# Gated linear attention feeding a feed-forward block: outputs of two head pairs at a time, a quarter of the TensorE array per head for the carried states

## The chip, the cores and the metric

The kernel runs on one core of a Trainium2 chip. The metric is the device time of one launch in microseconds (us), as the median of several runs. TensorE is called PE, VectorE DVE, ScalarE ACT, GpSimd POOL, SyncE SP.

## The reference

```python
def _attn_ref(q, k, v, f_logit):                       # each (4, 8, 768, 48)
    f = 1.0 / (1.0 + np.exp(-f_logit))
    for t in range(S):
        state = f[:, :, t, :, None] * state + np.einsum('bhd,bhe->bhde', k[:, :, t], v[:, :, t])
        y[:, :, t] = np.einsum('bhd,bhde->bhe', q[:, :, t], state)

def _moe_ref(x, w_in, w_out):                          # (3072, 384), (384, 2048), (2048, 384)
    h = x @ w_in
    g = np.where(h >= 1, h, np.where(h <= -1, 0.0, (h + 1) ** 2 / 4.0))
    return g @ w_out
```

The first part is a recurrence over 768 positions with a 48 x 48 state for each of 4 batches and 8 heads; its outputs, all heads side by side, are the rows x of the second part.

## The kernel before

**Steps, pairs, units.** The 768 positions are cut into 6 *steps* (`NI`) of 128. In each step the 8 heads are 4 *pairs* (`NP`), the two heads of a pair on rows 0 to 47 and 64 to 111 of a tile. Batches (`B` = 4) lie side by side in the free dimension. The feed-forward block of a step is 16 *units* (`NJ`) of 128 hidden columns. Unit u of the whole kernel (0 to 95) is IN, nine matmuls of x with `w_in` (line 205, tile `ph`), then the activation on ACT and DVE, then OUT, nine matmuls with `w_out` (line 229, tile `po`). Weights and x are split into a rounded high part and a remainder (`w_hi`, `w_lo`), hence three products for each.

**The attention of a pair in one step.** `gate` scans the forget gates on DVE (lines 399, 406) and multiplies k and q by them (408, 410). `scores` makes k·q for each head and batch (line 456), each on half of the array's rows, and `masks` multiplies by a triangle on DVE (467, tile `am`). `outputs` makes, for each batch, values times masked scores (line 514, one matmul for each head, each on half of the array's columns) and, from step 1 on, the carried state times q (lines 517 and 518, over all 112 rows against a block-diagonal tile `dbd`, again one half of the columns each). `states` makes k·v for the next step (564) from the transposed keys `kn`, transposed on PE (480) in steps 0 and 1 and on DVE (494) later. The decayed states are written into `dbd` by two DVE operations for a pair (441), one for each head; the new state is the sum of it and of `states`' result, two DVE operations (571).

**From outputs to x.** An output is rounded by ACT (528, the high part) and the remainder is made by DVE (544). In step 0 it is done otherwise: the output is computed a second time (521), PE subtracts the high part (540, tile `minus`) and ACT writes the remainder (541). The fourth pair has no row block of its own in x: its outputs go to tile `y3`, and six DMAs (`move`, half of them issued by SP and half by ACT; `x<-y` in the profile) carry them to rows 48 to 63 and 112 to 127 of the three x tiles. The first unit of a step waits for these six DMAs (`need = moved[i]`).

**Weights.** The weights arrive as 24 pieces of 64-bit words (`raw<-in_w`). Each is put together on DVE (308, 311, 313) and split into the high part (ACT, 322 or 320) and the remainder: on DVE (323), or, for every second piece from the seventh on, by an accumulating DMA issued on POOL (319). Units 0 to 3 need the first three pieces for IN, the next three for OUT, and so on.

**What sets the order.** Every operation is put into a `Plan` with a cost in ns (`COST`); a list scheduler gives each a start and the instructions are emitted in order of start, a fixed queue for each engine. PE's own order is the order of the calls. Where the plan leaves PE without work for over 0.7 us, `warm` puts in matmuls of zeros (line 283) for 0.7 of it. The calls of `scores` and `outputs` are put between units by a table:

```python
        at = 16 * (i - 1) + ((5, 8, 11, 14) if i == 1 else (1, 5, 9, 13))[m]
        before = 16 * (i - 1) + ((2, 5, 8, 11) if i == 1 else (-2, 1, 5, 9))[m]
```

`before` is the unit after which the pair's scores stand, `at` that after which its outputs and states stand. In steps 2 to 5 three of the four outputs of a step thus follow another pair's scores directly.

## Time and profile before

| | us |
|---|---|
| median of 3 runs | 520.79 |
| lowest and highest run | 518.71, 520.99 |
| the profiled execution's own time | 519.36 |
| its span, first to last instruction | 517.3 |

The granted TensorE clock of the profiled execution is 0.994 of full speed. In a page's rows `L205` is line 205, `ph<-x,w_hi` says which tile is written from which, and `x576` is the number of records. A matmul of plain fp32 operands (lines 456 to 564) leaves two records, one for each of its two passes; one of rounded operands (205, 229) leaves one. PEld is the weight load that goes ahead of a matmul. Times within the execution are counted from its first instruction.

### The profile page before, as it was taken

To read this page: it belongs to the slowest core of one execution; us is meant where nothing else is said; L and a number is where in the kernel's file an instruction comes from. 1 tells how busy PE (TensorE), PEld (TensorE's weight loads), DVE (VectorE), ACT (ScalarE), POOL (GpSimd) and SP (SyncE) were. 2 spreads that over 40 slices of the span, in tenths; PEclk is the share of its full clock that TensorE was granted. 3 is DMA by queue.
4 is the path that set the end of the run, shared out by engine and by line. 5 is a ranking of instruction groups with operands and counts; after the bars stand their busy time and mean duration, and the time that the engine had idled before them with its cause. 6 is when DMAs were issued, how large, how long until landed. Compare 5 with 4: busy or idle time off the path is not lost.

```text
span 517.3 us, 8421 instructions
## 1 busy us (share of the span) xinstructions
PE 501.5 (97%) x3295; PEld 407.0 (79%) x3295; DVE 390.6 (76%) x768; ACT 238.8 (46%) x389; POOL 31.0 (6%) x57
## 2 busy tenths in 40 slices
PE   7979999999999999999999999999999999999995
PEld 3747878887887888888888888888888888888883
DVE  7999999999999999998898798865655443433332
ACT  2347665654343453454443543534434434544542
POOL 3111111021100100010100010100000000000000
PEclk9899999999999999999999999999999999999999
DMA  8689687825401204412304512145522311100001
GB/s 283 200 238 322 182 250 195 240 71 132 129 25 52 77 22 97 158 29 91 116 24 117 163 58 98 41 140 154 177 90 82 114 50 30 63 1 1 0 1 67
DMA packets 22367, 56.65 MB, mean 110 GB/s; under 512 B 3504, under 2 KB 7088, under 8 KB 22320
## 3 DMA queue, kind: packets, MB, share of 16 engines
q1 hardware_dynamic: 19872, 51.31, 31.0%
q0 software_dynamic: 1296, 2.36, 2.8%
q10 hardware_dynamic: 1152, 2.37, 2.0%
q8 instruction: 28, 0.46, 0.4%
q14 instruction: 19, 0.16, 0.1%
HBM read 44.22 MB, written 4.72 MB: 95 GB/s over the span
## 4 chain that ended last, share of the span: by engine, by line
PE 76%; DVE 17%; DMA 4%; issue 1%; ACT 0%; SPq 0%; ACTq 0%; DVEq 0%
PE po L229 33%; PE ph L205 31%; PE pa L456 4%; PE pa L514 3%; DVE kn L494 3%; PE pa L518 3%; DMA raw<-in_w 2%; DVE glo L223 2%; DVE bits L313 2%; DVE bits L311 2%; DVE act L217 1%; DMA v<-in_v 1%; DVE am L467 1%; DVE w L399 1%; DVE w_lo L323 1%
## 5 line engine op out<-in xcount | busy, mean ns | idle before, releaser
L205 PE MATMUL ph<-x,w_hi 128*128 128x512 f32 x576 | 177.4, 389 | 0.0
L209 ACT ACTIVATE act<-ph,half 128x512 f32<-128x512 f32 x96 | 66.2, 689 | 145.1 <-PE ph L205 138.4
L205 PEld LDWEIGHTS ph<-x,w_hi 128*128 128x128 f32 x576 | 108.1, 188 | 22.5
L229 PE MATMUL po<-ghi,w_lo 128*128 128x512 f32 x288 | 115.8, 402 | 1.1 <-DMA w_lo<-bits 0.8
L205 PE MATMUL ph<-x,w_lo 128*128 128x512 f32 x288 | 112.4, 390 | 2.4 <-DMA x<-y 2.4
L217 DVE SCALAR_TENSOR_TENSOR act<-ph,act 128x512 f32<-128x512 f32 x96 | 65.9, 686 | 63.3 <-ACT act L212 62.8
L229 PE MATMUL po<-ghi,w_hi 128*128 128x512 f32 x288 | 112.5, 390 | 0.0
L220 ACT CAST ghi<-act 128x512 fp32r<-128x512 f32 x96 | 59.6, 620 | 82.0 <-DVE act L217 80.0
L229 PE MATMUL po<-glo,w_hi 128*128 128x512 f32 x288 | 83.2, 390 | 0.3 <-DVE glo L223 0.3
L223 DVE TENSOR_TENSOR glo<-act,ghi 128x512 fp32r<-128x512 f32 x96 | 65.9, 687 | 20.5 <-ACT ghi L220 19.1
L229 PEld LDWEIGHTS po<-ghi,w_lo 128*128 128x128 f32 x288 | 54.0, 188 | 15.3 <-ACT ghi L220 1.6
L205 PEld LDWEIGHTS ph<-x,w_lo 128*128 128x128 f32 x288 | 54.1, 188 | 14.2 <-DMA x<-y 2.9
L229 PEld LDWEIGHTS po<-glo,w_hi 128*128 128x128 f32 x288 | 53.9, 188 | 12.5 <-DVE glo L223 1.0
L229 PEld LDWEIGHTS po<-ghi,w_hi 128*128 128x128 f32 x288 | 54.1, 188 | 10.3
L212 ACT ACTIVATE act<-act 128x512 f32<-128x512 f32 x96 | 60.7, 632 | 2.9
L494 DVE STREAM_TRANSPOSE kn<-kq 32x128 f32<-32x128 f32 x192 | 58.1, 303 | 2.9
L467 DVE TENSOR_TENSOR am<-pa,mask 128x512 f32<-128x512 f32 x45 | 30.7, 686 | 17.1 <-PE pa L456 13.8
L514 PE MATMUL pa<-am,v 128*48 128x128 f32 (+1 forms) x368 | 36.8, 277 | 0.1
L517 PE MATMUL pa<-kq,dbd 112*64 112x128 f32 x160 | 30.6, 272 | 0.0
L518 PE MATMUL pa<-kq,dbd 112*48 112x128 f32 x160 | 30.6, 272 | 0.0
L456 PEld LDWEIGHTS pa<-kq 48*128 48x128 f32 x360 | 22.4, 188 | 8.9 <-issue 5.3
L456 PE MATMUL pa<-kq 48*128 48x128 f32 x360 | 27.0, 285 | 1.6 <-DVE kq L410 1.6
(87 smaller groups left out, 418.6 us busy)
## 6 DMA issues: line engine op xcount, KB each, us to landing
raw<-in_w SPq DMA_DIRECT2D x48, 512.0 KB, 3.5
kq<-in_kq SPq DMA_DIRECT2D x18, 512.0 KB, 4.5
v<-in_v SPq DMA_DIRECT2D x24, 192.0 KB, 4.0
out_y<-raw SPq DMA_DIRECT2D x18, 256.0 KB, 2.7
f<-in_f SPq DMA_DIRECT2D x16, 256.5 KB, 3.0
w_lo<-bits POOLq DMA_DIRECT2D x9, 256.0 KB, 5.2
kq<-kq ACTq DMA_DIRECT2D x18, 64.2 KB, 2.9
kq<-kq SPq DMA_DIRECT2D x18, 64.2 KB, 2.5
```

What stands on the lines that cost most here:

```text
L205: nc.tensor.matmul(ps, w_in(part, j, kt), xt[:, kt, t], start=(n == 0), stop=(n == 8))
L209: nc.scalar.activation(a, ps, AF.Relu, bias=half, scale=0.5)
L212: nc.scalar.activation(a, a, AF.Square)
L217: nc.vector.scalar_tensor_tensor(out=a, in0=ps, scalar=1.0, in1=a, op0=ALU.max, op1=ALU.min)
L220: nc.scalar.copy(hi, a)
L223: nc.vector.tensor_tensor(out=lo, in0=a, in1=hi.bitcast(F32), op=ALU.subtract)
L229: nc.tensor.matmul(po[e], w_out(part, j, e), g, start=(j == 0 and n == 0), stop=(j == NJ - 1 and n == 2))
L456: nc.tensor.matmul(ps[:, b], kt[a:z, B - 1 - b], qt[a:z, b], start=True, stop=True)
L467: o = vec("dve", lambda t=t, ps=ps: nc.vector.tensor_tensor(out=t, in0=ps, in1=mask.rearrange("u (o t) -> u o t", o=1).broadcast_to([C, B, ...
L494: nc.vector.transpose(kn[n % 2][u:u + 32, :, r:r + 32], src[:, :, u:u + 32])
L514: nc.tensor.matmul(ps[r:z, m], vb[:, a:a + z - r], t[:, m], start=True, stop=first)
L518: nc.tensor.matmul(ps[64:R, m], dt[:, m, 64:R], qt[:, m], start=False, stop=True)
```

## The change

- The heads are paired anew (`PAIRS`), so that two pairs give two whole x tiles: the first heads of both pairs one, the second heads the other.
- `outputs` is called once for two pairs. For each batch, four matmuls take the carried states with q: each 48 rows by 64 (or 48) columns, one for each head of the two pairs, in a quarter of the array each. Then come the values with the masked scores of all four heads, two columns' halves at a time as before.
- `states` is called once for two pairs, with 64 columns for a pair's first head; the new states of both pairs are one sum on DVE instead of four.
- `dbd` goes; the decayed states stand compactly in `ds`, written by one operation for a pair instead of two.
- In step 0 the second computation of the outputs, `minus` and the gathering DMAs go. `heads` computes the outputs of heads 0 to 5 straight into the three x tiles' layout, `thirds` adds the 16-column thirds of heads 6 and 7 there by 32-column matmuls, with one tiny closing matmul of zeros for each tile. The remainder is made by DVE, as in later steps. Values of step 0 come in two layouts of their own (`va`, 512 KB; `vb`, 640 KB); later steps load the values of two pairs in one DMA of 384 KB.
- The first unit waits for the three x tiles one at a time instead of for the DMAs.
- The table moves: scores of step 1 stand after units 2, 4, 8, 10 and its outputs after 7 and 13; from step 2 on scores after -2, 0, 5, 7 and outputs after 3 and 11, counted from the step before's first unit. Plan costs change, and zeros are put in where the plan leaves PE without work for over 0.5 us, for 0.9 of it.

```diff
+
+PAIRS = ((0, 2), (1, 3), (4, 6), (5, 7))
+
-COST = dict(mm=227, scores=1100, y0=1850, y=1850, states=500, turn=500, rows=317, scan=1145, dve=605, small=200, state=365,
+COST = dict(mm=227, scores=1100, y=2600, states=900, turn=500, rows=317, scan=1145, dve=605, small=200, state=300, sums=480,
...
-    v = tiles(4, [C, B, 2, D], F32, "v")
+    v_all = const.tile([C, 2 * B * 4 * D], F32, name="v")
+    v = [v_all[:, k * B * 4 * D:(k + 1) * B * 4 * D].rearrange("u (b h e) -> u b h e", b=B, h=4) for k in range(2)]
-    am = tiles(3, [C, B, C], F32, "am")
+    am = tiles(4, [C, B, C], F32, "am")
     kn = tiles(2, [C, B, C], F32, "kn")
-    dbd = tiles(2, [R, B, R], F32, "dbd")
-    state = const.tile([R, NP * B, D], F32, name="state")
+
+    sd = const.tile([128, NP * B * D + 2 * B * D + 16], F32, name="sd")
+    state, ds = sd[:R, 0:NP * B * D].rearrange("r (g e) -> r g e", e=D), sd[:R, NP * B * D:]
     act_f = tiles(2, [128, N + 1], F32, "act")
...
-    minus = const.tile([R, R], F32R, name="minus")
...
-    set_dbd = [add("POOL", 700, lambda t=t: fresh(t)) for t in dbd]
+    set_ds = add("POOL", 200, lambda: fresh(ds[:, 2 * B * D:]))
...
-    def bank(first):
-
-        count = 6 if first else 3
-        k = turn["n"] % count
-        turn["n"] += 1
+    def bank(k=None):
+
+        if k is None:
+            k = turn["n"] % 3
+            turn["n"] += 1
...
+    va = sd[:, 0:4 * B * 64].rearrange("u (b h e) -> u b h e", b=B, h=4)
+    vb = v_all[:, 0:B * 320].rearrange("u (b e) -> u b e", b=B)
...
-        c["lv"] = dma(v[n % 4], vv[i, p], 192, old(n - 4, "y", "st"))
+        if n % 2:
+            c["lv"] = att[n - 1]["lv"]
+        elif i == 0:
+            c["lv"] = dma(va if p == 0 else vb, vad if p == 0 else vbd, 512 if p == 0 else 640)
+        else:
+            c["lv"] = dma(v[k], vv[i, p // 2], 384, old(n - 4, "y", "st"), att[2]["st"])
...
-            for a, z in HEADS:
-                c["db"].append(vec("state", lambda a=a, z=z: nc.vector.tensor_tensor(
-                    out=dbd[k][a:z, :, a:z], in0=state[a:z, p * B:(p + 1) * B],
-                    in1=whole(kq[p])[a:z].rearrange("r (b o) -> r b o", o=1).broadcast_to([z - a, B, D]), op=ALU.mult),
-                    pf, state_of[i - 1, p], old(n - 2, "y", "se"), set_dbd[k]))
-
-    def scores(n):
+            c["db"].append(vec("state", lambda: nc.vector.tensor_tensor(
+                out=ds[:, n % 2 * B * D:(n % 2 + 1) * B * D].rearrange("r (b e) -> r b e", b=B), in0=state[:, p * B:(p + 1) * B],
+                in1=whole(kq[p])[:R].rearrange("r (b o) -> r b o", o=1).broadcast_to([R, B, D]), op=ALU.mult),
+                pf, state_of[i - 1, p // 2], old(n - 2, "y", "se"), set_ds))
...
+    def scores(n, at=(None, None)):
-        held = [bank(i == 0) for _ in HEADS]
+        held = [bank(k) for k in at]
...
-            t = am[(2 * n + h) % 3]
+            t = am[n % 2 * 2 + h]
-                c["sc"], ready["mask"], old(n - 2 + h, "y"))
+                c["sc"], ready["mask"], old(n - 2, "y"))
...
+    def rounded(b, yf, hi, lo, y, past):
+        eh = sca("act", lambda: nc.scalar.copy(hi, yf), y, past)
+        el = vec("dve", lambda: nc.vector.tensor_tensor(out=lo, in0=yf, in1=hi.bitcast(F32), op=ALU.subtract), eh)
+        banks[b] = [eh, el]
+        return [eh, el]
+
+        held = [bank(), bank()]
...
+        def emit():
+
+            for m in range(B):
+                for e, h in ((0, 0), (1, 1), (1, 0), (0, 1)):
+                    (r, z), q = HEADS[h], part(kq[p + e], 1)
+                    a = (e * B + m) * D
+                    nc.tensor.matmul(held[h][1][64 * e:(64, R)[e], m], ds[r:z, a:a + (64, 48)[e]], q[r:z, m], start=m == 0, stop=False)
+
+            for h, (_, ps, _) in enumerate(held):
+                for m in range(B):
+                    vm = vt[:, m].rearrange("u h e -> u (h e)")
+                    nc.tensor.matmul(ps[0:64, m], vm[:, h * D:h * D + 64], am[h][:, m], start=False, stop=m == B - 1)
+                    nc.tensor.matmul(ps[64:R, m], vm[:, (2 + h) * D:(3 + h) * D], am[2 + h][:, m], start=False, stop=m == B - 1)
+
+        y = c["y"] = d["y"] = add("PE", "y", emit, c["am"], d["am"], c["lv"], c["db"], d["db"], [b[2] for b in held])
+        xt = x[i % 2]
+        for t, (b, ps, _) in zip((p, p + 1), held):
+            hi, lo = (y3[:, 0], y3[:, 1]) if t == NT else (xt[:, t, 0], xt[:, t, 1])
+            past = [moved.get(i - 1)] if t == NT else [unit_in.get((i - 2, NJ - 1))]
+            x_of[i, t] = rounded(b, wide(ps)[:R], hi[:R], lo[:R], y, past)
+        if p > 0:
+
+            moved[i] = [move(k, xt[r:r + 16, t].bitcast(F32), y3[z + 16 * t:z + 16 * t + 16].bitcast(F32), x_of[i, NT], x_of[i, t])
...
+        def emit():
+            for e in range(2):
+                for m in range(B):
+                    for h, (r, z) in enumerate(((0, 64), (64, R))):
+                        a = (e * B + m) * D
+                        nc.tensor.matmul(ps[r:z, a:a + D], kn[e][:, B - 1 - m, r:z], vs[e][h](m), start=True, stop=True)
...
+        s = state[:, p * B:(p + 2) * B].rearrange("r b e -> r (b e)")
+        if i == 0:
+            o = sca("copy", lambda: nc.scalar.copy(s, ps[:R, 0:2 * B * D]), c["st"])
+        else:
+            o = vec("sums", lambda: nc.vector.tensor_tensor(out=s, in0=ps[:R, 0:2 * B * D], in1=ds[:, 0:2 * B * D], op=ALU.add),
+                    c["st"], c["db"], d["db"])
+        c["se"] = d["se"] = banks[b] = state_of[i, p // 2] = [o]
...
+    def heads(t, vs, a, deps, held=None):
+
+        ps = firsts[t][1]
         def emit():
             for m in range(B):
+                for e in range(2):
+                    nc.tensor.matmul(ps[64 * e:64 * e + 64, m], vs(m, e), a[e][:, m], start=m == 0, stop=False)
+
+        return add("PE", 870, emit, deps, held)
+    def thirds(t, a, deps):
...
+                for e in range(2):
+                    w = vb[:, m, 128 + 96 * e + 32 * t:160 + 96 * e + 32 * t]
+                    nc.tensor.matmul(ps[64 * e + 32:64 * e + 64, m], w, a[e][:, m], start=False, stop=False)
+
+            nc.tensor.matmul(ps[:, B - 1, C - 1:], zeros, zeros[:, 0:1], start=False, stop=True)
...
-        need = moved[i] if j == 0 else []
+        need = moved[i] if j == 0 and i > 0 else []
...
+        if u == 0:
+
+            n = 0
+            for kt in range(3):
+                for k, terms in ((0, ((w_lo, 0), (w_hi, 0))), (1, ((w_hi, 1),))):
+                    def some(kt=kt, terms=terms, n=n):
+                        for k, (part, t) in enumerate(terms):
+                            nc.tensor.matmul(s, w_in(part, j, kt), x[0][:, kt, t], start=(n + k == 0), stop=(n + k == 8))
+                    o = add("PE", len(terms) * COST["mm"], some, x_of[0, kt][k], split[kt])
+                    n += len(terms)
+            unit_in[i, j] = o
...
-    ready["minus"] = sca(200, lambda: nc.scalar.mul(minus, ident[:R, :R], -1.0), ready["ident"])
         prepare(n)
-        scores(n)
-        if n > 0:
-            outputs(n - 1)
-        if n > 1:
-            remainder(n - 2)
-        masks(n)
-    outputs(NP - 1)
-    remainder(NP - 2)
+        scores(n, ((0, 1), (2, 3), (0, 1), (3, 0))[n])
+        if n == 1:
+            for t in range(2):
+                att[0]["y"] = att[1]["y"] = heads(t, lambda m, e, t=t: va[:, m, 2 * e + t], am[t::2], [att[e]["am"][t] for e in range(2)], att[0]["lv"])
+        transpose_tensor(n, (1, 3)[n])
+    two = [att[n]["am"] for n in (2, 3)]
+    heads(2, lambda m, e: vb[:, m, 64 * e:64 * e + 64], am[0::2], [a[0] for a in two], [att[2]["lv"], att[1]["am"]])
+    for t in range(NT):
+        y = att[2]["y"] = att[3]["y"] = thirds(t, am[1::2], [a[1] for a in two])
+        x_of[0, t] = rounded(firsts[t][0], wide(firsts[t][1]), x[0][:, t, 0], x[0][:, t, 1], y, None)
+        u = 16 * (i - 1)
+        groups.setdefault(u + ((2, 4, 8, 10) if i == 1 else (-2, 0, 5, 7))[m], []).append((0, n))
+        if m % 2 == 0:
+            groups.setdefault(u + ((7, 13) if i == 1 else (3, 11))[m // 2], []).append((1, n))
...
-        if u == 1:
+        if u == 0:
+            states(0)
+        elif u == 1:
             for n in (2, 3):
                 transpose_tensor(n)
-            for n in (2, 3):
-                states(n)
+        elif u == 2:
+            states(2)
...
-                if o is unit_in[0, 0]:
-
-                    warm(int((o.start - idle) / 230) + 4)
-                elif idle and o.start - idle > 700:
-                    warm(int((o.start - idle) * 0.7 / (330 if o.start < 50000 else 230)))
+                if idle and o.start - idle > 500:
+                    warm(int((o.start - idle) * 0.9 / (330 if o.start < 10000 else 230)))
...
```

The order of PE's instructions before, in step 2: the end of one pair's outputs and its states, between the IN of one unit and the OUT of another (`pa` is the output bank, `v` values, `am` masked scores).

```order
L514 MATMUL pa_115<-am_81,v_73 64x128
L514 MATMUL pa_115<-am_79,v_73 48x128
L517 MATMUL pa_115<-kq_69,dbd_85 64x128
L518 MATMUL pa_115<-kq_69,dbd_85 48x128
L564 MATMUL pa_113<-v_73,kn_83 48x48 x8
L229 MATMUL po_118<-ghi_92,w_lo 128x512
```

PE's instructions of the change at the outputs of two pairs: one batch of each kind, and the first two of the states (`sd` holds the decayed states).

```order
L537 MATMUL pa_110<-kq_68,sd 64x128
L537 MATMUL pa_108<-kq_69,sd 48x128
L537 MATMUL pa_110<-kq_69,sd 48x128
L537 MATMUL pa_108<-kq_68,sd 64x128
...
L542 MATMUL pa_110<-am_76,v 64x128
L543 MATMUL pa_110<-am_78,v 48x128
...
L570 MATMUL pa_109<-v,kn_80 64x48
L570 MATMUL pa_109<-v,kn_80 48x48
```

Before, the four rows of lines 514 to 518 stand four times for one pair, so 32 matmuls for two pairs, and 16 for their states. In the change there are 16 of line 537, then 16 of lines 542 and 543, then 16 of line 570, in one block.

PE's instructions before, from the end of step 0's outputs to the first unit (`minus` is the negated identity, `ident,kq` the transposes).

```order
L540 MATMUL pa_114<-x_89,minus 112x512
L283 MATMUL ph_117<-zeros 128x512
L540 MATMUL po_118<-y_91,minus 112x512
L480 MATMUL po_119<-ident,kq_68 128x112 x4
L480 MATMUL po_120<-ident,kq_69 128x112 x4
...
L564 MATMUL pa_113<-v_72,kn_82 64x48
...
L205 MATMUL ph_116<-x_89,w_lo 128x512
```

The same place in the change.

```order
L500 MATMUL pa_109<-ident,kq_68 128x112 x4
...
L592 MATMUL pa_110<-am_76,v 64x128
...
L603 MATMUL po_114<-am_77,v 32x128
...
L605 MATMUL po_114<-zeros 128x1
L603 MATMUL po_115<-am_77,v 32x128
...
L605 MATMUL pa_110<-zeros 128x1
L629 MATMUL ph_111<-x_85,w_lo 128x512
L629 MATMUL ph_111<-x_85,w_hi 128x512 x2
```

The transposes now stand ahead of the last outputs, the first states behind the first unit, and the first unit follows the last of the `thirds` directly.

PE's instructions of the change in step 1's first scores and the OUT of unit 1 behind them; before, the transpose, the scores and the OUT stood there with no row of line 283 among them.

```order
L500 MATMUL pa_109<-ident,kq_68 128x112 x4
L287 MATMUL po_115<-zeros 128x512
...
L480 MATMUL pa_110<-kq_68 128x128
...
L233 MATMUL po_115<-ghi_89,w_hi 128x512
L287 MATMUL po_115<-zeros 128x512
...
L233 MATMUL po_113<-glo_91,w_hi 128x512
```

From the first unit to the OUT of unit 13 the change has 36 matmuls of zeros (two of them inside the first unit); before had none. From there to the end it has 4, and before had 6.

More of the change, by code (lines that the diff above doesn't have):

```diff
@@ L137, in gla_moe @@
 @with_exitstack
-def gla_moe(ctx: ExitStack, tc: tile.TileContext, ff, kqd, f0, vv, wd, maskd, identd, gates, values, headsd, out):
+def gla_moe(ctx: ExitStack, tc: tile.TileContext, ff, kqd, f0, vv, vad, vbd, wd, maskd, identd, gates, values, headsd, out):
     nc = tc.nc
@@ L496, in transpose_rows @@
         c["tr"] = c["kn"][-1]
+    def rounded(b, yf, hi, lo, y, past):
[3 more added lines that the diff above has]
+        return [eh, el]
     def outputs(n):
         i, p = pairs[n]
-        c = att[n]
-        b, ps, held = bank(i == 0)
-        first = i == 0
-        ms = [am[(2 * n + h) % 3] for h in range(2)]
-        qt, dt = part(kq[p], 1)[:R], dbd[n % 2]
@@ L523, in outputs @@
-        c["y"] = add("PE", "y0" if first else "y", emit, c["am"], c["lv"], c["db"], held, again and again[2])
-        xt = x[i % 2]
-        hi, lo = (y3[:, 0], y3[:, 1]) if p == NP - 1 else (xt[:, p, 0], xt[:, p, 1])
-        yf = wide(ps)
-        past = [moved.get(i - 1)] if p == NP - 1 else [unit_in.get((i - 2, NJ - 1))]
-        eh = sca("act", lambda: nc.scalar.copy(hi[:R], yf[:R]), c["y"], *past)
-        c["rest"] = b, again, yf[:R], hi[:R], lo[:R], eh
-        if not first:
-            remainder(n)
@@ L533, in remainder @@
-    def remainder(n):
-        i, p = pairs[n]
-        b, again, yf, hi, lo, eh = att[n]["rest"]
-        xt = x[i % 2]
-        if again:
-            y = wide(again[1])[:R]
-            o = add("PE", 300, lambda: nc.tensor.matmul(y, minus, hi, start=False, stop=True), eh, ready["minus"])
-            el = sca("act", lambda: nc.scalar.copy(lo, y), o)
-            banks[b], banks[again[0]] = [eh], [el]
-        else:
-            el = vec("dve", lambda: nc.vector.tensor_tensor(out=lo, in0=yf, in1=hi.bitcast(F32), op=ALU.subtract), eh)
-            banks[b] = [eh, el]
-        x_of[i, p] = [eh, el]
-        if p == NP - 1:
-            moved[i] = [move(k, xt[r:r + 16, t].bitcast(F32), y3[z + 16 * t:z + 16 * t + 16].bitcast(F32), eh, el, x_of[i, t])
-                        for t in range(NT) for k, (r, z) in enumerate(((48, 0), (112, 64)))]
@@ L561, in emit @@
+    firsts = [bank(k) for k in (4, 5, 2)]
+    def heads(t, vs, a, deps, held=None):
+        ps = firsts[t][1]
         def emit():
             for m in range(B):
-                for h, (r, z) in enumerate(rows):
-                    nc.tensor.matmul(ps[r:z, m, :D], kn[n % 2][:, B - 1 - m, r:z], v[n % 4][:, m, h], start=True, stop=True)
-        c["st"] = add("PE", "states", emit, c["kn"], c["lv"], held)
-        s = state[:, p * B:(p + 1) * B]
-        if i == 0:
-            c["se"] = [sca("copy", lambda: nc.scalar.copy(s, ps[:R, :, :D]), c["st"])]
-        else:
-            c["se"] = [vec("state", lambda r=r, z=z: nc.vector.tensor_tensor(
-                out=s[r:z], in0=ps[r:z, :, :D], in1=dbd[n % 2][r:z, :, r:z], op=ALU.add), c["st"], c["db"]) for r, z in HEADS]
```

85 lines of the change are left out of this document (43 added, 42 removed).

## The prediction, made before the change was run

> **What bounds the kernel now.** First the top of the page and its two rows of tenths, then two stretches (busy time of PE, PEld, DVE, ACT and POOL, granted clock, DMA share, GB/s), then PE's waits.
>
> ```profile
> span 517.3 us, 8421 instructions
> ...
> PE 501.5 (97%) x3295; PEld 407.0 (79%) x3295; DVE 390.6 (76%) x768; ACT 238.8 (46%) x389; POOL 31.0 (6%) x57
> ...
> PE   7979999999999999999999999999999999999995
> ...
> DVE  7999999999999999998898798865655443433332
> ```
>
> ```profile
> 100.00:120.00 20.00, 20.00 (x158) 16.61 (x154) 19.79 (x36) 10.69 (x18) 3.51 (x4) 1.00 0.49 136
> ...
> 320.00:360.00 40.00, 40.00 (x274) 33.16 (x273) 27.40 (x54) 17.92 (x28) 1.31 (x2) 1.00 0.33 98
> ```
>
> ```profile
> PE ph L205 <- DMA x<-y: 2.4, 1, 2.4
> ...
> PE po L229 <- DMA w_lo<-bits: 0.8, 1, 0.8
> ```
>
> There are three stages. Until the first unit PE waits and is filled with zeros; the longest wait is for the gathered outputs. From there to about 120 us PE and DVE are both full (20.00 and 19.79 of 20). After that PE alone is full and DVE has room (27.4 of 40). So a PE microsecond saved late is a microsecond of the total; one saved at the start is worth it only as far as DVE follows.
>
> **The late stage, steps 2 to 5.** PE's rows at a pair's outputs and states alone, at scores alone, and in the last step at the last pair's outputs:
>
> ```profile
> 191.12 0.61 PE L205 MATMUL ph<-x,w_hi 128*128 128x512 f32 x2
> 191.66 0.43 PE L514 MATMUL pa<-am,v 128*64 128x128 f32 x4
> ...
> 193.25 0.27 PE L518 MATMUL pa<-kq,dbd 112*48 112x128 f32 x1
> 193.25 0.27 PE L517 MATMUL pa<-kq,dbd 112*64 112x128 f32 x1
> 193.36 0.27 PE L518 MATMUL pa<-kq,dbd 112*48 112x128 f32 x1
> 193.37 0.27 PE L517 MATMUL pa<-kq,dbd 112*64 112x128 f32 x1
> 193.47 0.53 PE L564 MATMUL pa<-v,kn 128*48 128x48 f32 x16
> 193.93 0.50 PE L229 MATMUL po<-ghi,w_lo 128*128 128x512 f32 x1
> 194.26 0.40 PE L229 MATMUL po<-ghi,w_hi 128*128 128x512 f32 x1
> ```
>
> ```profile
> 198.23 1.16 PE L456 MATMUL pa<-kq 48*128 48x128 f32 x16
> 199.32 0.50 PE L229 MATMUL po<-ghi,w_lo 128*128 128x512 f32 x1
> ```
>
> ```profile
> 430.84 0.43 PE L514 MATMUL pa<-am,v 128*64 128x128 f32 x4
> ...
> 432.75 0.50 PE L229 MATMUL po<-ghi,w_lo 128*128 128x512 f32 x1
> ```
>
> The chain of waits gives the blocks in which scores and outputs stand together, with states and, in the last step, without:
>
> ```profile
> 212.63 1.09 PE pa L456 x16
> 215.98 2.27 PE po L229 x9
> 218.25 2.04 PE ph L205 x9
> ...
> 411.37 1.09 PE pa L456 x16
> 414.37 2.26 PE po L229 x9
> ```
>
> Scores alone take 1.09 (198.23 to 199.32), outputs and states alone 2.27, of which the outputs 1.81 and the states 0.46; all three 3.35 (212.63 to 215.98); without states 3.00, and the last pair's outputs 1.91. Each interruption also costs about 0.2 at its edges: 0.31 from the start of the last IN matmul (191.35, the second of the two) to 191.66, and 0.33 from 193.93 to 194.26, where nine undisturbed matmuls take 2.04, 0.23 each. Steps 2 to 4 each have five interruptions: 1.09 + 3 x 3.35 + 2.27 + 5 x 0.2 = 14.4. The last has 1.09 + 3 x 3.00 + 1.91 + 1.0 = 13.0.
>
> The change has six interruptions, four of scores and two of outputs. In the rows of lines 517 and 518 both column halves start a pass together, 0.11 apart from pass to pass: a slot. Two pairs now need 16 slots for values (1.81, as for one pair before) and, for the carried states, 16 matmuls of two passes in four quarters: 8 slots, 0.88, if the quarters run side by side; before, the two pairs had 16. A change of array form adds some 0.2: the scores' 8 slots are 0.88 but take 1.09. The states of two pairs have the form of step 0's, first head 64 wide:
>
> ```profile
> 32.65 1.13 PE L564 MATMUL pa<-v,kn 128*64 128x48 f32 x32 [1.23 <-ACT kn L483]
> 33.71 2.55 PE L283 MATMUL ph<-zeros 128*128 128x512 bf16 x11
> ```
>
> These 32 passes take about 1.0 (32.65 to 33.71 with the edge), where twice 0.46 stood before: the wider weights give nothing back. The block's two output banks are held until ACT and DVE have rounded both tiles; `states` takes the third bank, and the next scores stand two or more units later, so nobody waits for that. A block is 0.88 + 0.2 + 1.81 + 0.95 = 3.85, a step 4 x 1.09 + 2 x 3.85 + 6 x 0.2 = 13.3, so three steps save 1.1 each; the last step has 4.36 + 2 x 2.9 + 1.2 = 11.4 and saves 1.6. Zeros: 6 before, 4 now, at 0.23 each (11 in 2.55): 0.5. Together 3.3 + 1.6 + 0.5 = 5.4. The gather in these steps now starts after unit 11 instead of 13 and stays hidden. The unknown is the quarters: no row has them. At no gain at all (16 slots) the late stage loses 8 blocks x 0.88 of it, 7.0, and ends 1.6 worse than now; nothing below 8 slots is possible, since each quarter has 8 passes.
>
> The Trainium skill, "TensorE: Matmul & The Clock Gate", Part 3 on packing small matmuls, says that matmuls start and end strictly in program order. By that rule a matmul's second pass would hold up the next quarter's first, two quarters would work at a time, and these 16 matmuls would take 16 slots, 1.76. The trace speaks against it as far as two halves show it: the order has line 517 first, yet at 193.25 a pass of 518 starts, ahead of the second pass of 517 at 193.37. No run here shows quarters in any order, so the rule stays as a rival.
>
> **The start.** Before, in step 0:
>
> ```profile
> 22.73 1.16 PE L456 MATMUL po<-kq 48*128 48x128 f32 x14 [0.34 <-ACT x L541]
> ...
> 29.09 0.48 PE L540 MATMUL po<-y,minus 112*112 112x512 f32 x1
> ...
> 38.65 0.50 PE L205 MATMUL ph<-x,w_lo 128*128 128x512 f32 x1 [2.39 <-DMA x<-y]
> ```
>
> From the last remainder's matmul to the first unit lie 9.6 us: a copy, six DMAs and their landing. They go. The last scores end at 23.9 in both (the gather of k and q ahead of them stays). What then follows, with these durations:
>
> ```profile
> L467 DVE TENSOR_TENSOR am<-pa,mask 128x512 f32<-128x512 f32 x45 | 30.7, 686 | 17.1 <-PE pa L456 13.8 <-PE pa L514 3.2
> L528 ACT CAST x<-pa 112x512 fp32r<-112x512 f32 x17 | 9.9, 585 | 4.1 <-PE pa L518 4.1
> L544 DVE TENSOR_TENSOR x<-pa,x 112x512 fp32r<-112x512 f32 x15 | 10.2, 678 | 0.0
> ```
>
> Two masks (0.69 each) end at 25.4. The third of the `heads` and the three `thirds` are 8 slots each and a change of form, 1.1: with two transposes in front they start near 25.5 and end at 30.0. Rounding the last tile takes 0.59 + 0.68 and two hand-overs, so the first unit, which waits for the tiles one by one, ends near 32.0. Before it ended at 38.65 + 2.04 = 40.7. Gain 8.7; earliest 31 (no change of form), latest 35, if the masks stand behind pieces on DVE, or the third piece's high part behind the two key copies that now stand ahead of it on ACT.
>
> **Step 1 gives most of that back.** OUT of unit 13 waits for one of the last pieces:
>
> ```profile
> 115.84 0.68 DVE L323 TENSOR_TENSOR w_lo<-bits,w_hi 128x512 fp32r<-128x512 f32 x1
> ...
> 116.63 0.50 PE L229 MATMUL po<-ghi,w_lo 128*128 128x512 f32 x1
> ```
>
> The piece is ready at 116.52, PE starts 0.11 later, at the end of its own queue. Both are full. From unit 0's end PE has 27 more INs and OUTs (nine at 2.04, 55.1) and 75.9 in all (40.7 to 116.63), so 20.8 of attention. The change has there five scores (6.5), two double blocks (8.1), 24 transposes (2.4, a slot each), step 0's states in two pieces (2.3) and 34 zeros at 0.23 (7.8): 27.1, 6.3 more. OUT of unit 13 comes at 32.0 + 55.1 + 27.1 = 114.2. The zeros stand for waits on DVE that the plan foresees, and cover 0.9 of them; the tenth that is left, 0.8, I add: 115.0, 1.6 earlier than before.
>
> DVE could follow that far. Its rows:
>
> ```profile
> L441 DVE TENSOR_TENSOR dbd<-state,kq 48x192 f32<-48x192 f32 x40 | 14.0, 350 | 0.6
> L571 DVE TENSOR_TENSOR state<-pa,dbd 48x192 f32<-48x192 f32 x32 | 11.3, 352 | 0.7 <-PE pa L564 0.4
> ```
>
> ```profile
> DVE bits L308 <- DMA raw<-in_w: 1.0, 1, 1.0
> DVE kq L408 <- DMA kq<-in_kq: 0.9, 1, 0.9
> ```
>
> In step 1 the decays go from 8 to 4 (1.4 less) and the sums from 8 to 2 larger ones (2.8 less 2 x 0.56, an estimate between 0.35 for 192 elements and 0.68 for 512); step 0's three remainders add 2.0. Net 1.1 less, and 1.9 more if the two waits for DMAs go. So OUT of unit 13 comes at best 3.0 earlier, and if SP holds a piece up, not at all: the values of step 1 now wait on SP for the second states, with a piece's load queued behind. Step 0's values grow from four DMAs of 192 KB to 512 and 640 KB (the code's figures), 384 KB more ahead of the first pieces; DVE has step 0's masks to do meanwhile, so I take nothing, and the latest start above holds it. Steps 2 to 5 lose another 2.9 of DVE time each or nearly so, which hides under PE and counts for nothing.
>
> **Sum.** 1.6 + 5.4 = 7.0 off 519.36, the profiled execution: 512.4. That execution lies 1.4 below the median of 520.79; the runs spread over 2.3, so I add nearly half of it: 513.0.
>
> **Rivals.** *The quarters do not run side by side.* Place: the first 16 matmuls of each of the ten double blocks. For it: no row shows four at once. Against it: both column halves (517, 518) run at full pace together, and the two row halves of the scores do (16 passes in 1.09). Two at a time cost 8 slots more in each block, 8.8: 521.8, level or just above; one at a time, 24 slots more, 26.4: 539.4. It decides from about 14 slots on, where 10 x 6 x 0.11 eats the gain. Chance 0.13, of which 0.05 one at a time.
>
> *Step 1 stays where it was.* DVE or a late piece sets OUT of unit 13, at 116.6 to 120 as PE stands behind zeros and then still waits. For it: DVE's 19.79 of 20. Against it: PE hardly waits there now. 514.6 to 518. Chance 0.19.
>
> *The start gives more than I count.* The first unit ends at 31, DVE's two waits for DMAs are gone, so OUT of unit 13 comes the full 3.0 earlier (1.4 more), and the quarters need no change of form (10 x 0.2): 509.6. For it: the two column halves follow 128-row work here with only 0.1 at the edge. Against it: the scores' 1.09. Chance 0.10.
>
> **Numbers.** The forecast, 511 to 515, has 0.58. The range from 509 to 520 leaves out the turn-taking quarters and most of the two-at-a-time case. A measurement here can tell about 0.5%, 2.6 us. Faster by more: 0.58 + 0.10 + 0.15 of the second rival = 0.83. Within: 0.04 + 0.08 = 0.12. Slower: 0.05.
>
> **What would show it.** Right: a double block near 3.85 in steps 2 to 4, its first part near 0.9 to 1.1; first unit's last matmul near 32; OUT of unit 13 near 115; no wait of PE for a DMA of x at the first unit. Wrong: the block's first part at 1.8 or more; PE waits for pieces between zeros; a first unit after 35.

## The result and the profile after

The changed kernel takes 512.3 us (median of 4 runs, 511.61 to 512.67), the kernel before 520.88 (median of 4, 518.71 to 520.99): ratio 0.984, 95% interval 0.981 to 0.987. The profiled execution took 512.57 us, 6.8 less than that of before (519.36).

From the top of the changed kernel's page: the span, the engines, and the tenths of PE and DVE. Then the same two stretches as before (busy time of PE, PEld, DVE, ACT and POOL, granted clock, DMA share, GB/s), and PE's waits.

```profile
span 510.8 us, 8368 instructions
...
PE 500.1 (98%) x3305; PEld 399.1 (78%) x3305; DVE 377.6 (74%) x727; ACT 235.2 (46%) x381; POOL 30.9 (6%) x56
...
PE   8999999998999999999999999999999999999995
...
DVE  7999999997999999679979869965654453433332
```

```profile
100.00:120.00 20.00, 20.00 (x178) 16.41 (x176) 18.95 (x34) 9.55 (x16) 3.49 (x6) 1.00 0.57 149
...
320.00:360.00 40.00, 40.00 (x277) 33.12 (x276) 27.59 (x45) 17.75 (x29) 2.62 (x4) 1.00 0.39 116
```

```profile
PE po L233 <- ACT ghi L224: 1.5, 1, 1.5
PE po L233 <- DVE glo L227: 0.8, 1, 0.8
```

PE's wait for the gathered x (2.4) is gone. The pattern is the old one: PE full, DVE full to about 120 us and with room after that. (In the kernel after, L209 and L629 are the IN matmuls, L233 the OUT, L287 the zeros, L480 the scores, L537 the carried states, L542 and L543 the values, L570 the states.)

The start, PE's rows in order of time:

```profile
25.02 1.09 PE L592 MATMUL pa<-am,v 128*64 128x128 f32 x16
...
28.26 1.07 PE L603 MATMUL pa<-am,v 128*32 128x128 f32 x16
...
32.00 1.13 PE L570 MATMUL pa<-sd,kn 128*64 128x48 f32 x32
```

The third of the `heads` and the three `thirds` follow each other 1.03 to 1.1 apart, and the first unit's last matmul leaves PE free at 32.00, the moment forecast.

The late stage, from the chain of waits: scores, and a double block with its neighbours.

```profile
205.29 1.09 PE pa L480 x16
...
217.14 2.04 PE ph L209 x9
219.18 1.03 PE pa L537 x24
220.21 0.25 PE pa L542
...
222.10 0.92 PE pa L570 x31
223.02 2.27 PE po L233 x9
```

The block's first part, the 16 carried-state matmuls of two pairs, takes 1.03: eight slots and an edge. The values go from 220.21 to 222.10 (1.9), the states take 0.92. With both edges a block costs 4.06 in all eight places that have states, 3.14 in the two of the last step, and scores alone 1.31.

Where the gain comes and goes, as the start of the same work in the two profiled executions (us; a row of each unit's first matmul):

| | before | after | earlier by |
|---|---|---|---|
| OUT of unit 0 | 45.54 | 35.94 | 9.6 |
| OUT of unit 2 | 55.55 | 48.28 | 7.3 |
| OUT of unit 3 | 59.63 | 59.95 | -0.3 |
| OUT of unit 8 | 88.74 | 88.51 | 0.2 |
| OUT of unit 13 | 116.63 | 115.88 | 0.8 |
| IN of unit 16 | 124.50 | 123.92 | 0.6 |
| IN of unit 32 | 205.58 | 203.09 | 2.5 |
| IN of unit 48 | 286.17 | 282.27 | 3.9 |
| IN of unit 64 | 366.00 | 361.11 | 4.9 |
| IN of unit 80 | 443.08 | 436.66 | 6.4 |

Most of the early lead goes at one place, between OUT of unit 2 and OUT of unit 3. There stand, in the changed kernel:

```profile
49.65 1.47 PE L287 MATMUL po<-zeros 128*128 128x512 bf16 x6
51.88 0.96 PE L233 MATMUL po<-glo,w_hi 128*128 128x512 f32 x3 [0.76 <-DVE glo L227]
...
55.20 1.69 PE L287 MATMUL po<-zeros 128*128 128x512 bf16 x7
56.72 0.55 PE L500 MATMUL pa<-ident,kq 112*128 112x112 f32 x4
57.10 1.25 PE L287 MATMUL po<-zeros 128*128 128x512 bf16 x5
58.28 1.56 PE L480 MATMUL pa<-kq 48*128 48x128 f32 x16
59.95 0.50 PE L233 MATMUL po<-ghi,w_lo 128*128 128x512 f32 x1
```

With two more at 52.68 these are twenty zeros in ten microseconds. What they cover is the question for the experiments.

### The profile page after: what moved, and what is told of

The parts are those of the page before. It is cut to its first block, busy times and chain, and to the rows that moved or that the text cites. A ratio compares the mean times of both kernels' runs of the same rounds, so it can differ in the third digit from the quotient of the medians.

```text
span 510.8 us, 8368 instructions
## 1 busy us (share of the span) xinstructions
PE 500.1 (98%) x3305; PEld 399.1 (78%) x3305; DVE 377.6 (74%) x727; ACT 235.2 (46%) x381; POOL 30.9 (6%) x56
## 3 DMA queue, kind: packets, MB, share of 16 engines
q10 hardware_dynamic: 1056, 2.17, 1.9%
## 4 chain that ended last, share of the span: by engine, by line
PE 78%; DVE 12%; DMA 5%; issue 2%; ACT 1%; SPq 0%; ACTq 0%; DVEq 0%
PE po L233 35%; PE ph L209 32%; PE pa L480 3%; PE pa L543 2%; DMA raw<-in_w 2%; DVE bits L317 2%; PE pa L537 2%; DVE bits L319 1%; DMA x<-y 1%; DVE w L405 1%; PE pa L570 1%; DVE f L412 1%; DVE bits L314 1%; DVE act L221 1%; DMA f<-in_f 1%
## 5 line engine op out<-in xcount | busy, mean ns | idle before, releaser
L209 PE MATMUL ph<-x,w_hi 128*128 128x512 f32 x570 | 175.5, 389 | 0.0
L209 PEld LDWEIGHTS ph<-x,w_hi 128*128 128x128 f32 x570 | 107.0, 188 | 22.3
L233 PE MATMUL po<-ghi,w_lo 128*128 128x512 f32 x288 | 116.4, 404 | 1.6 <-ACT ghi L224 1.5
L233 PE MATMUL po<-ghi,w_hi 128*128 128x512 f32 x288 | 112.4, 390 | 0.0
L209 PE MATMUL ph<-x,w_lo 128*128 128x512 f32 x285 | 111.2, 390 | 0.0
L233 PE MATMUL po<-glo,w_hi 128*128 128x512 f32 x288 | 83.4, 391 | 0.8 <-DVE glo L227 0.8
L233 PEld LDWEIGHTS po<-ghi,w_lo 128*128 128x128 f32 x288 | 54.0, 188 | 16.2 <-ACT ghi L224 3.0
L233 PEld LDWEIGHTS po<-glo,w_hi 128*128 128x128 f32 x288 | 53.9, 188 | 13.2 <-DVE glo L227 1.6
L209 PEld LDWEIGHTS ph<-x,w_lo 128*128 128x128 f32 x285 | 53.5, 188 | 11.3
L233 PEld LDWEIGHTS po<-ghi,w_hi 128*128 128x128 f32 x288 | 54.1, 188 | 10.2
L480 PEld LDWEIGHTS pa<-kq 48*128 48x128 f32 x368 | 23.8, 187 | 8.2 <-issue 6.0
L480 PE MATMUL pa<-kq 48*128 48x128 f32 x368 | 28.5, 285 | 0.0
L405 DVE TENSOR_TENSOR_SCAN w<-f,ones 128x512 f32<-128x512 f32 (+1 forms) x18 | 20.8, 1158 | 2.0 <-ACT f L403 2.0
L412 DVE TENSOR_TENSOR_SCAN f<-f,rec 128x512 f32<-128x512 f32 (+1 forms) x18 | 20.8, 1162 | 0.5
L403 ACT ACTIVATE f<-f 128x513 f32<-128x513 f32 (+2 forms) x18 | 10.9, 608 | 22.1 <-DMA f<-in_f 18.0
```

Source lines behind the costliest of these rows:

```text
L209: nc.tensor.matmul(ps, w_in(part, j, kt), xt[:, kt, t], start=(n == 0), stop=(n == 8))
L233: nc.tensor.matmul(po[e], w_out(part, j, e), g, start=(j == 0 and n == 0), stop=(j == NJ - 1 and n == 2))
L405: s1 = vec(1200 // count, lambda b0=b0, b1=b1, u0=u0, u1=u1: nc.vector.tensor_tensor_scan(out=wide(w[:, u0:u1]), data0=ft[:, b1 * C:b0 * C ...
L412: s2 = vec(1200 // count, lambda fwd=fwd, b0=b0, b1=b1: nc.vector.tensor_tensor_scan(out=fwd, data0=fwd, data1=wide(rec[:, b0:b1]), initia ...
L480: nc.tensor.matmul(ps[:, b], kt[a:z, B - 1 - b], qt[a:z, b], start=True, stop=True)
```

## The experiments

Two theories to tell apart on step 1. Mine: PE and DVE are both full there, the zeros only fill waits on DVE, so the early start is worth what DVE can follow. The rival: PE's own queue sets the pace, the zeros are work in it. On the late stage: four quarters side by side, or only two. Each was run beside the kernel before on one chip: e1, e2, e6 and e7 on one, e3, e4, e5 and e8 on a second, e9 to e12 on a third. So the ratios compare across the table, while the change itself was run again on the third chip alone. OUT of unit 13 is that of the one profiled execution, the median that of all runs:

| run | median us | ratio to before, 95% | OUT of unit 13 |
|---|---|---|---|
| the change, run again (e11) | 512.9 | 0.985 (0.982 to 0.988) | 115.66 |
| no zeros after unit 0 (e1) | 513.59 | 0.986 (0.982 to 0.990) | 118.75 |
| unit 0 late by 9.1 (e2) | 522.2 | 1.004 (1.002 to 1.006) | 124.55 |
| 18 pieces by ACT and DMA (e6) | 516.57 | 0.992 (0.990 to 0.995) | 120.89 |
| e6 without zeros (e7) | 516.75 | 0.993 (0.991 to 0.996) | 120.22 |
| DVE lighter by 16.5, no zeros (e8) | 513.28 | 0.987 (0.985 to 0.989) | 115.96 |
| later scores in step 1 (e9) | 512.92 | 0.986 (0.983 to 0.989) | 115.89 |
| values' loads later (e12) | 512.31 | 0.985 (0.981 to 0.988) | 115.29 |
| two quarters at a time (e3) | 520.42 | 0.999 (0.996 to 1.001) | 117.28 |
| one quarter at a time (e5) | 528.11 | 1.014 (1.011 to 1.017) | 118.24 |
| states 48 wide (e4) | 514.19 | 0.990 (0.987 to 0.992) | 115.64 |
| e9 and e4 together (e10) | 511.22 | 0.983 (0.980 to 0.986) | 116.55 |

**e1, the zeros taken out.** `begun` turns true at the first unit.

```diff
-                if idle and o.start - idle > 500:
+                if idle and o.start - idle > 500 and not begun:
```

> The changed kernel without the 40 filler matmuls after the first unit (some 9.1 us of PE at 0.227 each). My theory (in step 1 the zeros only stand where PE would wait for DVE, which sets the pace until the last pieces of weights): PE waits where the zeros stood, OUT of unit 13 stays at 114.5 to 116 and the total within 1.5 us of the change's 512.3. Rival (PE's own queue sets the pace, the zeros are work in it): OUT of unit 13 comes 6 to 8 us earlier, near 109, and the total falls to 504 to 506. Third way: the idle PE is granted a lower clock, and the total rises above 514 with a clock below 0.99 in some slice of step 1.

PE's rows at the same place, and its stretches (as above, with the granted clock ahead of the DMA share):

```profile
52.00 0.98 PE L233 MATMUL po<-glo,w_hi 128*128 128x512 f32 x3 [1.97 <-DVE glo L227]
...
56.41 0.60 PE L500 MATMUL pa<-ident,kq 112*128 112x112 f32 x4 [1.39 <-DVE kq L414]
58.21 2.67 PE L480 MATMUL pa<-kq 48*128 48x128 f32 x16 [1.20 <-DVE am L487]
...
61.40 0.63 PE L233 MATMUL po<-ghi,w_hi 128*128 128x512 f32 x1
61.83 0.63 PE L233 MATMUL po<-ghi,w_lo 128*128 128x512 f32 x1
```

```profile
40.00:60.00 20.00, 15.40 (x109) 11.81 (x109) 19.53 (x34) 11.39 (x21) 3.19 (x4) 0.95 0.65 199
60.00:80.00 20.00, 20.00 (x163) 16.50 (x160) 17.49 (x32) 11.30 (x20) 2.37 (x4) 0.88 0.74 207
```

At these three places zeros stood; now PE waits, each time for DVE, and each piece of work begins within 0.4 of where it began with zeros (52.00 for 51.88, 56.41 for 56.72, 58.21 for 58.28). So the rival falls: the zeros there are no work that could be saved. The third way came true in part: after those waits the same matmuls follow 0.43 apart instead of 0.23, the granted clock is 0.95 and 0.88 in two stretches, the scores take 2.67 instead of 1.56, and OUT of unit 13 is 2.9 later, outside the 114.5 to 116 that I had expected. The profiled execution lost all of it (515.48 against 512.57); the median, 513.59, lies about 1 us above the change and below the 514 of the third way, within the scatter told of under e11. The Trainium skill, "TensorE: Matmul & The Clock Gate", in the section on why this matters for kernels, asks for no idle gap of PE over some 3 us, lest the clock falls. Here three gaps of 1.2 to 2.0 us within eight were enough; in e5 a single one of 1.89 us was.

**e2, the first unit 9.1 us later.**

```diff
+                if o is first_in[0]:
+                    warm(40)
```

> The changed kernel with 40 filler matmuls (9.1 us) just ahead of the first unit, which so ends near 41 again as before the change. My theory (DVE, and with it the last pieces, set OUT of unit 13; an early start is given back): the total rises by 0 to 2.5 us, 512.3 to 514.8, and OUT of unit 13 stands at 116 to 118. Rival (PE's queue sets the pace from the first unit on): the total rises by the full 9.1, to 521.4, and OUT of unit 13 stands near 125.

My expectation fell. The total rose by 9.3 to 9.9, the whole delay, as the rival had it. That does not decide for the rival, since DVE was held up as well. DVE's row after the delay:

```profile
42.34 0.69 DVE L221 SCALAR_TENSOR_TENSOR act<-ph,act 128x512 f32<-128x512 f32 x1 [8.77 <-ACT act L216]
```

In DVE's queue the work on unit 0 has its fixed place ahead of the next pieces. DVE waits 8.77 for the late unit with everything behind it. In the kernel before, DVE worked on pieces through the same time (18.20 busy of 20 from 20 to 40 us, here 13.19), because the order was planned for a late first unit. From OUT of unit 0 to OUT of unit 13 it is 71.1 us before, 79.9 after, 79.8 in e2: the early start and the longer road belong to one order, and the start cannot be priced by itself.

**e6 and e7, nine more pieces taken off DVE,** e7 also without zeros.

```diff
-        moving = k >= 6 and k % 2
+        moving = k >= 6
```

> The changed kernel with the low parts of 18 pieces, not 9, made by ACT and an accumulating DMA: DVE has 9 x 0.68 = 6.1 us less to do in step 1, ACT some 5.5 more; the planned order puts 55, not 40, zeros after the first unit (3.4 us more of PE). My theory (DVE is the bound of step 1): OUT of unit 13 comes 3 to 6 us earlier as far as PE's queue lets it, total 507 to 510. Rival (PE's own queue is the bound): no earlier, with 15 more zeros up to 3.4 later, 512 to 516.

> Both edits: 18 pieces moved off DVE and no zeros after the first unit. My theory (DVE bounds step 1, and zeros cover only waits): about as the one with more pieces moved and zeros kept or up to 2 us less, 506 to 509. Rival (PE alone bounds step 1): the same time as without zeros alone, so that the moved pieces bring nothing beside it.

Both were slower than the change by some 4, against my theory as I had put it; e7 was slower than e1 too, which neither theory had. But neither is a clean test: the planner filled the room. By OUT of unit 13 the durations of DVE's instructions add up to 125.0 us in e6 (121.7 in the change), among them three more scans, a second sum and five transposes of step 2, and 53 zeros stand before it instead of 34. So an order was tried here, not a lighter DVE.

**e8, DVE lighter with every place kept.** The operation keeps its entry in the plan and issues nothing; the run also leaves out the zeros, as e1 does.

```diff
-        v = vec("dve", lambda: nc.vector.scalar_tensor_tensor(
-            out=t, in0=hw, scalar=0xC0000000, in1=t, op0=ALU.bitwise_and, op1=ALU.bitwise_or), v)
+        v = vec("dve",
+            lambda: None, v)
```

> The kernel without zeros after the first unit, and with the third operation of each of the 24 pieces of weights left out (the one that puts the sign back, 0.69 each, so all weights are positive), the places of everything else in the queues kept: DVE has 16.5 us less to do before OUT of unit 13. My theory (DVE is what step 1 waits for; the zeros cost nothing because they only fill that wait): OUT of unit 13 comes 6 to 10 us earlier than without zeros alone (118.8), at 109 to 113, and the total is 504 to 508. Rival (something other than DVE holds step 1, PE's own work or the loads of the pieces): within 2 us of the one without zeros, 511.5 to 514.

By the total the rival was right: 513.28 lies in its range, 0.3 below e1. OUT of unit 13 came 2.8 earlier than in e1, of 6 to 10 expected, for 16.5 us less on DVE, and even that is not all DVE's: OUT of unit 0 stood 0.8 earlier, and the granted clock was 0.97 and 0.94 from 40 to 60 and from 60 to 80 us, where e1 had 0.95 and 0.88 (by an estimate from these, up to 1.6 of the 2.8). PE's waits from unit 0 to OUT of unit 13 add up to 6.1, in e1 to 6.0. DVE itself is busy only 66.2 of the 80 us from 40 to 120. So DVE's load alone does not hold step 1. The largest wait that is left on PE there, at OUT of unit 7, and rows of DVE and ACT ahead of it:

```profile
84.37 0.50 PE L233 MATMUL po<-ghi,w_lo 128*128 128x512 f32 x1 [2.14 <-ACT ghi L224]
```

```profile
75.55 1.23 DVE L412 TENSOR_TENSOR_SCAN f<-f,rec 128x512 f32<-128x512 f32 x1
...
80.60 0.68 DVE L221 SCALAR_TENSOR_TENSOR act<-ph,act 128x512 f32<-128x512 f32 x1
```

```profile
73.35 0.63 ACT L216 ACTIVATE act<-act 128x512 f32<-128x512 f32 x1
...
80.80 0.69 ACT L213 ACTIVATE act<-ph,half 128x512 f32<-128x512 f32 x1 [4.63 <-PE ph L209]
...
83.28 0.52 ACT L503 COPY kn<-pa 128x448 f32<-128x448 f32 x1
83.71 1.14 ACT L224 CAST ghi<-act 128x512 fp32r<-128x512 f32 x2
```

Unit 7's square is ready at 73.98, but its place on DVE is behind two operations on a piece, the rest of a gate, two remainders and a sum, at 80.60. Its cast on ACT then stands behind the next unit, for which ACT idles 4.63, behind two operations on a piece and a key copy. So here the entry that PE needs is held by its place in two queues, not by how much DVE has to do.

**e9, step 1's scores one or two units later; e12, the loads of its values later.**

```diff
-        groups.setdefault(u + ((2, 4, 8, 10) if i == 1 else ...
+        groups.setdefault(u + ((3, 5, 9, 11) if i == 1 else ...
```

```diff
-            c["lv"] = dma(v[k], vv[i, p // 2], 384, old(n - 4, "y", "st"), att[2]["st"])
+            c["lv"] = dma(v[k], vv[i, p // 2], 384, old(n - 4, "y", "st"), att[2]["st"], piece[8 if n == NP else 14] if i == 1 else None)
```

> The changed kernel with step 1's four scores after units 3, 5, 9 and 11 instead of 2, 4, 8 and 10; 14 zeros fewer stand after the first unit (26, not 40). My theory, as far as it stands (between OUT of units 2 and 3 PE waits, mostly behind zeros, for the gate of the second scores, because the scores were put a unit earlier than before the change): OUT of unit 3 comes 3 to 6 us earlier, some of it is given back at the later scores, OUT of unit 13 comes 1 to 2.5 us earlier and the total is 1 to 2.5 us below the change run again here. Rival (the whole work of DVE, ACT and the loads up to the last piece sets OUT of unit 13): OUT of unit 13 and the total within 0.7 us of the change.

> The changed kernel with the two loads of step 1's values (384 KB each) put behind three and behind seven more pieces in SP's queue; PE's plan is the same but for a few rows. My theory (the piece that DVE waits for at 48.2, 0.99 us, is late because the loads of values stand ahead of it on SP and share its bandwidth): that wait goes, OUT of units 3 to 9 comes about 1 us earlier; OUT of unit 13 by 0 to 1, total 511.3 to 512.5. Rival (DVE has other work to do or the piece is late for want of its buffer): no change anywhere.

In e9 the gap goes: OUT of unit 3 comes at 54.26, 5.7 earlier, and OUT of unit 9 is still 3.8 ahead. OUT of unit 13 comes at 115.89, at the change's time to 0.02. The rival was right there: moving work along step 1 does not bring its last pieces earlier. Behind them something did change in the profiled execution: OUT of unit 14 follows 4.27 after OUT of unit 13 (5.87 in the change, 4.23 before it), without a wait, so IN of unit 16 comes 1.6 earlier and that execution took 511.02. The median does not show it. In e12 DVE's waits for pieces shrink from 1.2 to 0.4 between 36 and 120 us, OUT of units 3 to 9 comes 0.4 to 0.7 earlier, of 1 expected, OUT of unit 13 0.4 to 0.6, and the total cannot be told from the change.

**e11, the change itself once more,** for the comparison on one chip.

> The changed kernel itself, for the comparison on one chip: 0.984 of the kernel before, 511.5 to 513.5.

Its profiled execution took 515.47, 2.9 more than the first one of the same kernel, though OUT of unit 13 came 0.2 earlier. The difference arises at the next unit. PE's row and ACT's, in the first profiled execution of the change, then in this one:

```profile
121.75 0.50 PE L233 MATMUL po<-ghi,w_lo 128*128 128x512 f32 x1 [1.50 <-ACT ghi L224]
```

```profile
120.00 0.51 ACTq L251 DMA_DIRECT2D x<-y  x1
120.56 0.63 ACT L403 ACTIVATE f<-f 128x513 f32<-128x513 f32 x1 [3.47 <-DMA x<-y]
...
121.09 0.60 ACT L224 CAST ghi<-act 128x512 fp32r<-128x512 f32 x1
```

```profile
123.42 0.80 PE L233 MATMUL po<-ghi,w_lo 128*128 128x512 f32 x1 [3.38 <-ACT ghi L224]
```

```profile
121.66 0.51 ACTq L251 DMA_DIRECT2D x<-y  x1
122.22 0.63 ACT L403 ACTIVATE f<-f 128x513 f32<-128x513 f32 x1 [5.75 <-DMA f<-in_f]
...
122.76 0.60 ACT L224 CAST ghi<-act 128x512 fp32r<-128x512 f32 x1
```

The last of the gather's three DMAs on ACT's queue goes out only at 120.00 or 121.66, and the cast of unit 14 stands behind it. PE loses 1.5 or 3.4, and after the longer wait the granted clock falls. From 120 to 140 us, in the first execution and in this one:

```profile
120.00:140.00 20.00, 18.50 (x105) 14.72 (x107) 17.73 (x45) 9.48 (x16) 0.00 (x0) 1.00 0.21 64
```

```profile
120.00:140.00 20.00, 16.62 (x78) 13.38 (x78) 14.92 (x35) 9.06 (x15) 0.00 (x0) 0.91 0.25 72
```

The clock is 1.00 and 0.91. That issue waits for the first of the three, which carries the same completion semaphore: issued at 113.10 and 113.28, the first lands 6.9 and 8.4 later, at 119.98 and 121.64, and the third goes out 0.02 after that. The same 0.02 stands in e12, e3 and e5. Why the landing takes 6.9 once and 8.4 the other time is open, and no run put the gather on another queue. In e9, where PE does not wait at unit 14, all three go out between 117.64 and 119.44, ahead of the cast at 119.48. These two executions part here; that the spread of the other runs, 511.6 to 515.5, has the same cause is likely and not shown. One run says little about a difference of 2 us.

**e3 and e5, the quarters in another order.**

```diff
-            for m in range(B):
-                for e, h in ((0, 0), (1, 1), (1, 0), (0, 1)):
+            for m, e, h in [(m, *eh) for two in (((0, 0), (1, 1)), ((1, 0), (0, 1))) for m in range(B) for eh in two]:
```

```diff
-            for m in range(B):
-                for e, h in ((0, 0), (1, 1), (1, 0), (0, 1)):
+            for m, e, h in [(m, *eh) for eh in ((0, 0), (1, 1), (1, 0), (0, 1)) for m in range(B)]:
```

> The changed kernel with the carried states' matmuls in another order: all four of two quarters in turn (first head of the first pair and second head of the second), then all four of the other two. My theory (the four quarters run side by side, 8 slots of 0.11 in all): now at most two quarters have work at a time, 16 slots, 0.88 more in each of ten double blocks; a block in steps 2 to 4 goes from 4.06 to 4.94, the total from 512.3 to 521.1. Rival (PE takes matmuls as far ahead as it likes, so their order does not matter): no change, 512.3. Rival of the prediction (two at a time already): no change either, but then e5 costs little as well.

> The changed kernel with the carried states' matmuls quarter after quarter, four of each in turn. My theory (a matmul starts in order, but waits only for its own quarter, not for the end of the one before): three times six slots before the next quarter can begin, then eight, 26 slots for 8, so 18 x 0.11 = 2.0 more in each of ten blocks and 20 in all: 532. Strictly one at a time: 24 slots more, 538.7. Free order: 512.3.

The carried states and the row after them, in the change, in e3 and in e5:

```profile
219.11 1.10 PE L537 MATMUL pa<-kq,sd 48*64 48x128 f32 x32
220.14 0.32 PE L542 MATMUL pa<-am,v 128*64 128x128 f32 x1
```

```profile
225.24 1.59 PE L537 MATMUL pa<-kq,sd 48*64 48x128 f32 x32
226.76 0.32 PE L542 MATMUL pa<-am,v 128*64 128x128 f32 x1
```

```profile
226.37 2.54 PE L537 MATMUL pa<-kq,sd 48*64 48x128 f32 x32
228.83 0.32 PE L542 MATMUL pa<-am,v 128*64 128x128 f32 x1
```

And the first passes in e5, from 226.36 to 226.87 us (shortest, median and longest in ns, then the forms):

```profile
L537 PE MATMUL pa<-kq,sd x6: 269/269/320, 226.4 to 226.9; 48*64 48x128 f32 x5, 48*48 48x128 f32 x1
```

From first to next row 1.03, 1.52 and 2.46, with the same 32 passes. So the four quarters do run side by side, and their order matters: a whole block takes 4.06, 4.55 and 5.50. The size was off. The extra 0.49 and 1.43 are 4.5 and 13 slots, where I had 8 and 18. In e5 the second quarter's first pass (the one of 48 columns above) starts at 226.86, 0.49 after the first quarter's, when that quarter has started five of its eight passes. In e3 the second two quarters likewise start 0.50 after the first two. So PE starts a matmul while an earlier one in its queue, for a quarter that is taken, has not started (one in e5, two in e3). The prediction's rival from the Trainium skill ("TensorE: Matmul & The Clock Gate", Part 3, matmuls strictly in program order) is refuted by these rows. The totals follow: ten blocks lose 4.9 and 14.3, the medians against the change run again, on another chip, 7.5 and 15.2. In its profiled execution e3 loses another 2.4 between OUT of units 13 and 14 (8.3 there, 5.9 in the change), the place shown under e11; there the cast of unit 14 stands behind the load of f, which lands at 124.35. One of e5's four runs took 1796.99 us and is left out; nothing here shows why.

**e4 and e10, the states from 48 columns,** e10 with e9's scores.

```diff
-                    for h, (r, z) in enumerate(((0, 64), (64, R))):
+                    for h, (r, z) in enumerate(((0, 64), (64, R)) if i == 0 else HEADS):
```

> The changed kernel with the states of steps 1 to 4 made from 48, not 64, columns of the first head's keys (the 16 rows between the heads, which nothing reads, are left as they are). My theory (the pass of the states lasts as long as its weights take to load, 0.058 for 64 columns and 0.045 for 48): 16 passes x 0.013 = 0.2 less in each of eight blocks, 1.7 in all, 510.6; a block in steps 2 to 4 goes from 4.06 to 3.85. Rival (the second half's 48 columns or the form of the array sets the pace): no change, 512.3.

> Both that brought something or should: step 1's scores later, and the states of steps 1 to 4 from 48 columns (0.2 less in each of eight blocks, 1.6). If the two add, 2.5 to 4 us below the change run again here; if the later scores bring nothing, 1.3 to 1.8 below it.

The states and the row after them, in the change and in e4:

```profile
221.94 1.09 PE L570 MATMUL pa<-v,kn 128*48 128x48 f32 x32
222.95 0.50 PE L233 MATMUL po<-ghi,w_lo 128*128 128x512 f32 x1
```

```profile
221.41 0.89 PE L570 MATMUL pa<-v,kn 128*48 128x48 f32 x32
222.23 0.50 PE L233 MATMUL po<-ghi,w_lo 128*128 128x512 f32 x1
```

1.01 and 0.82: the block costs 3.86 instead of 4.06, as expected. The timed runs of e4 (511.45 to 515.91) do not show the 1.6 us; the scatter of e11 is larger. e10, with both edits, has the lowest median, 511.22, or 1.7 below the change run on the same chip, which is what I had expected if the later scores bring nothing; but the two intervals overlap (0.980 to 0.986, 0.982 to 0.988). So it is not shown to be faster than the change.

## Why the prediction came out right, step by step

*The start.* First unit's end forecast 32.0, measured 32.00. The exact hit is luck: the `thirds` ended at 29.3, not 30.0, and then PE was not held by the rounding of the last tile, as I had it, but had nine matmuls and two zeros to do, 2.7 without a wait.

*The double block.* Forecast 3.85 and an edge of 0.2, so 4.05; measured 4.06 with states, and 3.14 without (forecast 2.9 + 0.2). Its first part, 1.03, lies at the forecast of 0.88 to 1.1. Scores 1.31, forecast 1.29. This was the term with the most weight, and e3 and e5 show that its reason holds: side by side, or else 0.49 and 1.43 more in each of ten blocks. The rival's price of 8.8 for two at a time was not put to the test: in e3 the second two quarters start before the first two are done, and it costs 4.9 by its blocks.

*Steps 2 to 5.* Forecast 5.4. From OUT of unit 13 to IN of unit 80 the gain grows from 0.75 to 6.42: 5.7. By steps it is 1.9, 1.4, 1.0 and 1.5, where I had 1.1, 1.1, 1.1 and 1.6, and 0.5 for zeros.

*Step 1.* Forecast: nearly all of the early gain given back, OUT of unit 13 at 115.0. Measured 115.88, so 0.8 of 1.6 was left; here the size was off, half way to the rival in which step 1 stays where it was. The waits from unit 0 to OUT of unit 13 were rightly counted, 34 zeros and 0.9 of bare waits (I had added 0.8). PE's own work there was 0.8 more than counted, 83.0 instead of 82.2; two of the five scores took 1.56 and 1.35 instead of 1.09. What I had not seen is the wait of 1.5 at unit 14, behind the gather on ACT, of which the third part waits for the first to land: I had looked at the gather only in the later steps, where it stays hidden, and not at its issues in ACT's queue in step 1. By IN of unit 16 the gain has shrunk by only 0.2, since the kernel before has a wait of 0.82 and three zeros at the same place.

*The reason given for step 1* holds in part. The zeros stand for waits on DVE (e1: they turn into such waits at the same times). But "worth only as far as DVE follows" named one engine, and the runs name the order: a later start costs its full length (e2), a DVE with 16.5 us less to do brings at most 2.8 (e8), and scores moved by a unit bring 5.7 at unit 3 and nothing at unit 13 (e9). What would bring OUT of unit 13 earlier stays open; a new order of DVE, ACT and SP together was not tried.

*The sum.* 7.0 forecast for the profiled execution, 6.8 measured; the median 513.0 forecast, 512.3 measured. That the sum is so close is in part luck, since misses cancel: step 1 gave 0.8 less by OUT of unit 13, steps 2 to 5 gave 0.3 more, and 0.4 that nobody had counted arises behind the last unit's IN.

## What to carry to other kernels

Price an edit in the stage where one engine alone is full, and slot by slot: that gave 5.4 against 5.7, while a lead of 9.6 at the start came to 0.8. Where several in-order queues were planned together, neither the load of one engine nor the earlier start of another was a lever by itself; test with the order kept, and look which queue holds the entry that PE waits for, DMA issues on a compute engine's queue included. Before taking filler work out, look at what stands there without it: a wait of the same length, and a lower clock behind it.
